# Fewer, wider transfers for stacks, local scores and sums, a planner's clock threshold of 0.5, and new order tables in a four-layer attention kernel

## The chip, the cores and the metric

The kernel runs on one core of one Trainium2 chip. The metric is the device time of one execution in microseconds (us), the median over several runs. All traces are of one profiled execution.

## The reference

Four layers in the order A, B, A, B over x of shape [1, 2048, 512], with 32 heads of 16. Each layer adds the attention of the normalised x to x:

```python
# A: each position sees 8 keys, itself and every second one before it
idx = arange(S)[:, None] - arange(8)[None, :] * 2        # masked where < 0
attn = softmax(where(idx >= 0, q . k[idx] * 16 ** -0.5, -1e9))
oA = (attn . v[idx]) @ wo
# B: each position sees the 256 positions up to itself
p = softmax(where((i - j >= 0) & (i - j < 256), q . k * 16 ** -0.5, -1e9))
oB = (p . v) @ wo
x = x + A(layernorm(x)); x = x + B(layernorm(x))         # twice, same weights
```

Everything is float32.

## The kernel before, in words

The 2048 rows are cut into eight chunks of 256. An A layer and the B layer behind it go through the chunks together, so there are 16 pairs of steps in all, scopes A0, B0 to A15, B15. Matrices are split into a float16 high and a low part, and three products (L1034 to L1036 for transposed results, L1054 to L1057 for others) stand for one float32 product.

In a step of layer A, TensorE makes queries and keys and then local scores for a window of 39 keys per group of 32 rows (L1193). ScalarE copies them out (`keep`, L1202), `shelve` (L1211) writes them to a DRAM copy `sd`, and `band` (L1215) reads the diagonal band back into `l`, from which the softmax of eight weights follows (L1234 to L1251). The weights go through DRAM once more (`ptd`, `ptt`, L1278 and L1285) and meet the values (`vd`, `vs`, L1265 and L1273).

In a step of layer B, queries and keys (s = 0 and s = 1) come out transposed. ScalarE makes the high part `eh` (L1331), VectorE the low part `el` (L1334). Six transfers per operand (`put`, L1344, 128 KB each, z = 0 to 2 by two parities) write them to a DRAM copy `re`, and four `stack` tasks read it into `stk_q` (L1357) or `stk_k` (L1359), with the three parts of a head below each other in 48 rows. Rows 48 to 63 of each half are padding, filled once at the start; two of them in `stk_q` later hold the maxima. The first scores (L1420) run on the stacks. VectorE blanks a triangle (`pick`, L1439) and takes row maxima (L1435), which go through small DRAM tiles `md` (`mput`, L1471, and `mget`, L1477) into the pad rows of `stk_q`. Then the scores are made again with the maxima subtracted (L1571), ScalarE takes the exponentials (L1581, L1593), POOL or VectorE zeroes triangles (L1610, L1604), and the products with the values follow (L1626). At the end of a step the sums are collected from `os` (`gather`, L1700), inverted, sent out (L1710) and read back spread over 16 rows (`spread`, L1715).

What runs when is set by a planner. Every piece of work is a task, `plan.add(engine, us, function, r=reads, w=writes, size=KB, alt=other engine)`. The table `ORDER` holds for each scope and task its place in its engine's queue; a negative place chooses the alternative engine. `Plan.order` (L549) walks the queues with the tasks' assumed times and emits them in the order of their planned starts, so it also decides how the five queues interleave. In it a transfer lands after

```python
dma = max(dma, t.end + 0.9) + t.size / 390.0
landed = dma + 0.9 + SLACK[t.size < 50]
```

and `cool` makes TensorE slower where a stretch of `GRID` = 3.4133 us was filled by less than `LOW`:

```python
h[2] = 1.0 / (1.0 + math.exp((h[0] / GRID - LOW) / EDGE))
```

`RECORDS` corrects the number of profiler records of some tasks; 122 idle tasks of three matmuls (L1763) fill gaps of TensorE. Transfers are issued by SyncE and ScalarE and use eight semaphores in turn, so that a transfer's issue also waits for the transfer eight places before it.

Of the kernel before, what the change touches and what calls it, by code (L numbers as in the profile page):

```python
# [9 lines left out]
F16 = mybir.dt.float16  # L10
# [435 lines left out]
SLOW = 0.25  # L446
LEAVE = {"Q": 0.1, "C": 0.13, "X": 0.18, "V": 0.14, "R": 0.1, "F": 0.095, "": 0.0}
AGAIN = {"PE": 0.0, "DVE": 0.11, "ACT": 0.12, "POOL": 0.055, "SP": 0.0}
GRID, LOW, EDGE = 3.4133, 0.4, 0.03
SLACK = 0.9, 0.45  # L450
SUPPLY = 5.0

# [228 lines left out]
def kernel(  # L681
# [1051 lines left out]
    def zeros(pad):  # L1733
        return pad.t.rearrange("p a b -> p (a b)").bitcast(F16)
# [70 lines left out]
```

## Time and profile before

| | before |
|---|---|
| median of 3 runs | 1408.19 us (1407.26 to 1411.21) |
| profiled execution, own time | 1414.15 us |
| its span | 1412.4 us |
| mean granted TensorE clock | 0.974 |
| busy: PE / PEld / DVE / ACT / POOL | 1308.5 / 841.8 / 852.2 / 825.8 / 405.9 us |
| DMA packets, bytes | 203658, 195.08 MB |

Busy time of an engine counts its instructions but not the issuing of transfers. PE is TensorE's matmuls, PEld its weight loads. The profiled execution took 6 us more than the median of the runs. In the page, a name such as stk_q<-re is a transfer or an operation that writes stk_q from re; SPq and ACTq are the queues of SyncE and ScalarE when they issue transfers.

### The profile page before, as it was taken

The page shows a single profiled execution, that of the slowest core. Times are in us where ns is not written, and L with a number is a line of the kernel's source. Part 1 is how long each engine was busy: PE and PEld are TensorE (multiplying, and loading weights), DVE is VectorE, ACT ScalarE, POOL GpSimd, SP SyncE. Part 2 cuts the span into 40 slices and gives each one's busy share as a digit, 9 for nine tenths or more (in the row PEclk, how much of TensorE's full clock was granted, in tenths as well). Part 3 has the DMA queues.
Part 4 walks back from the last instruction along what each step waited for, and adds up shares of the span by engine and source line. Part 5 has one row for each costly group of instructions (what it writes and reads, how often), then busy time and mean ns, then how long its engine had stood idle before and what let it go on. Part 6 is the DMA issues. An engine that isn't in the chain of part 4 may idle for free.

```text
span 1412.4 us, 62375 instructions
## 1 busy us (share of the span) xinstructions
PE 1308.5 (93%) x27206; PEld 841.8 (60%) x27206; DVE 852.2 (60%) x1932; ACT 825.8 (58%) x1303; POOL 405.9 (29%) x839
## 2 busy tenths in 40 slices
PE   8989999999898999879999898989999898998988
PEld 7766556575475746646566464746656474574645
DVE  5455764755647666374664637566473765748494
ACT  7754657474574746546676373838557364663644
POOL 5260212332221233133223130323242241222232
PEclk9999999999899998999999999999999999999999
DMA  8875544736355373552545546364554636335332
GB/s 261 236 168 162 133 115 135 154 114 171 102 148 134 88 200 92 148 147 86 160 113 152 152 143 158 94 174 125 157 123 134 175 100 155 102 98 147 103 98 67
DMA packets 203658, 195.08 MB, mean 138 GB/s; under 512 B 92892, under 2 KB 147932, under 8 KB 203384
## 3 DMA queue, kind: packets, MB, share of 16 engines
q1 hardware_dynamic: 175096, 170.43, 44.2%
q10 hardware_dynamic: 28288, 20.66, 6.0%
q8 instruction: 213, 3.49, 1.1%
q14 instruction: 61, 0.50, 0.1%
HBM read 94.11 MB, written 79.36 MB: 123 GB/s over the span
## 4 chain that ended last, share of the span: by engine, by line
PE 59%; DMA 11%; DVE 10%; ACT 7%; SPq 4%; issue 4%; POOL 2%; ACTq 1%; DVEq 0%; POOLq 0%
PE banks L1034 7%; PE banks L1626 7%; PE banks L1035 6%; PE banks L1036 6%; PE banks L1056 5%; PE banks L1054 5%; PE banks L1571 4%; PE banks L1057 4%; PE banks L1420 4%; DVE m L1435 3%; PE banks L1193 3%; PE banks L1302 3%; ACT p L1581 2%; DMA stk_q<-re 2%; DVE banks L1439 1%
## 5 line engine op out<-in xcount | busy, mean ns | idle before, releaser
L1435 DVE TENSOR_REDUCE m<-banks 128x2 f32<-128x512 f32 x448 | 302.1, 688 | 8.4
L1581 ACT ACTIVATE p<-banks,sclB 128x896 f32<-128x896 f32 x224 | 221.0, 1007 | 74.3 <-PE banks L1571 51.5
L1439 DVE COPY_PREDICATED banks<-trm,banks 128x128 f32<-128x128 int16 x448 | 124.2, 291 | 120.8 <-PE banks L1420 111.8
L1610 POOL TENSOR_SCALAR_AFFINE_SELECT ps<-ps 64x256 f32<-64x256 f32 x300 | 118.2, 416 | 252.3 <-ACT ps L1593 231.2
L1610 POOL TENSOR_SCALAR_AFFINE_SELECT p<-p 64x256 f32<-64x256 f32 x264 | 103.1, 412 | 214.7 <-ACT p L1581 206.6
L1420 PE MATMUL banks<-stk_k,stk_q 48*64 48x320 f16 (+4 forms) x2560 | 139.5, 274 | 24.5 <-DVE m L1435 7.0
L1571 PE MATMUL banks<-stk_q,stk_k 64*64 64x256 f16 (+3 forms) x3584 | 121.0, 239 | 25.0 <-DMA stk_q<-md 8.4
L1420 PEld LDWEIGHTS <-stk_q 48*64 48x64 f16 x2560 | 65.7, 107 | 107.5 <-issue 94.8
L1571 PEld LDWEIGHTS <-stk_k 64*64 64x64 f16 x3584 | 70.3, 108 | 91.0 <-issue 74.3
L1593 ACT ACTIVATE ps<-banks,sclB 128x768 f32<-128x768 f32 x112 | 100.2, 899 | 40.7 <-PE banks L1571 28.4
L1626 PE MATMUL banks<-p,v 64*32 64x192 f32 (+1 forms) x3584 | 112.6, 355 | 6.1 <-ACT p L1581 1.8
L1202 ACT COPY s<-banks 128x624 f32<-128x624 f32 x64 | 74.7, 1257 | 40.7 <-PE banks L1193 23.1
L1640 DVE TENSOR_TENSOR os<-os,banks 128x256 f32<-128x256 f32 x112 | 45.7, 416 | 83.4 <-ACT os L1643 67.0
L1334 DVE SCALAR_TENSOR_TENSOR el<-banks,eh 128x512 f16<-128x512 f32 x64 | 42.8, 687 | 79.4 <-ACT eh L1331 74.0
L1626 PEld LDWEIGHTS banks<-p,v 64*32 64x32 f32 x3584 | 62.9, 106 | 37.6 <-issue 13.0
L1643 ACT COPY os<-banks 128x256 f32<-128x256 f32 x112 | 40.8, 370 | 70.6 <-PE banks L1626 54.4
L1034 PE MATMUL banks<-xh,wA1h 128*128 128x256 f16 x256 | 72.1, 282 | 4.1 <-ACT v L1369 4.1
L1034 PE MATMUL banks<-xh,wA0h 128*128 128x256 f16 x256 | 71.9, 281 | 0.6 <-ACT v L1369 0.6
L1035 PE MATMUL banks<-xl,wA1h 128*128 128x256 f16 x256 | 71.7, 280 | 0.0
L1036 PE MATMUL banks<-xh,wA1l 128*128 128x256 f16 x256 | 71.5, 279 | 0.0
L1035 PE MATMUL banks<-xl,wA0h 128*128 128x256 f16 x256 | 71.3, 279 | 0.0
L1036 PE MATMUL banks<-xh,wA0l 128*128 128x256 f16 x256 | 71.1, 278 | 0.0
(216 smaller groups left out, 3063.8 us busy)
## 6 DMA issues: line engine op xcount, KB each, us to landing
sd<-s SPq DMA_DIRECT2D x92, 156.0 KB
ptt<-ptd SPq DMA_DIRECT2D x128, 96.0 KB
stk_k<-re SPq DMA_DIRECT2D x128, 96.0 KB
stk_q<-re SPq DMA_DIRECT2D x128, 96.0 KB
vs<-vd SPq DMA_DIRECT2D x64, 156.0 KB
re<-eh SPq DMA_DIRECT2D x75, 128.0 KB
vd<-ve SPq DMA_DIRECT2D x32, 256.0 KB
xm<-y SPq DMA_DIRECT2D x32, 256.0 KB
```

Of the source, the lines that this page charges most:

```text
L1034: nc.tensor.matmul(ps[mp].t[:, i], wh, xh, start=k == 0, stop=False)
L1035: nc.tensor.matmul(ps[mp].t[:, i], wh, xl, start=False, stop=False)
L1036: nc.tensor.matmul(ps[mp].t[:, i], wl, xh, start=False, stop=k == 3)
L1202: nc.scalar.copy(S_.t.rearrange("p k (s r) -> p r s k", r=4)[:, 2 * i : 2 * i + 2], pbs[i].t[:, :, 0 : 8 * WIN].rearrange("p r (s k) -> p ...
L1420: nc.tensor.matmul(o, lhs, k, start=True, stop=True, tile_position=(64 * par, 64 * h))
L1435: nc.vector.tensor_reduce(out=m.t[:, :, u, qb], in_=ps.t[:, :, 0 : 2 * P], op=ALU.max, axis=AX.X)
L1439: nc.vector.copy_predicated(t[:, :, 0:64], trm[:, 0].bitcast(I16).unsqueeze(1).broadcast_to([P, 2, 64]), t[:, :, C : C + 64])
L1571: nc.tensor.matmul(ps.t[64 * h : 64 * h + 64, par, at + x0 : at + x0 + q1 - q0], stk[hf, kt][r, col, k0 : k0 + 64], stk[hf, 0][r, col, q0: ...
L1581: nc.scalar.activation(big.t[:, 2 * i : 2 * i + 2], ps.t[:, :, 0:448], AF.Exp, scale=scl["B", 1])
L1593: nc.scalar.activation(small.t.rearrange("p (i m) x -> p m i x", i=2), ps.t[:, :, 0:384].rearrange("p m (i x) -> p m i x", i=2), AF.Exp, s ...
L1610: E.affine_select(out=v, in_=v, pattern=[[0, 4], [a, 64]], compare_op=op, fill=0.0, base=0, channel_multiplier=-a)
L1626: nc.tensor.matmul(acc.t[32 * mm : 32 * mm + 32, h, q0:q1], vv[r, 17 * (H * blk + hd) : 17 * (H * blk + hd) + 32], x.t[r, mm, x0 : x0 + q1 ...
```

## The change

Four transfers get other shapes, the planner's threshold changes, and all tables of places are new. The counts of transfers fall from 1664 to 1391; TensorE's instructions are the same in kind and number.

```diff
-GRID, LOW, EDGE = 3.4133, 0.4, 0.03
+GRID, LOW, EDGE = 3.4133, 0.5, 0.03
 ...
 ORDER = {
-    "B3": [259, 261, 269, 270, 81, 82, 83, 275, 774, 278, 312, 273, 765, 276, 311, 785, 791, 792, 793, 796, 797, 802,
+    "B3": [257, 259, 266, 267, 80, 81, 82, 272, 774, 278, 316, 270, 764, 273, 313, 790, 792, 793, 799, 800, 801, 802,
 ...
# local scores
-            sd = buf("dram", [4, 32 * (WIN + 1) * H], F32, "sd", f"sd{l}_{c}_{t}")
+            sd = buf("dram", [P, WIN * H], F32, "sd", f"sd{l}_{c}_{t}")
             def shelve(E, S_=S_, sd=sd):
-                for g in range(4):
-                    E.dma_start(sd.t[g, 0 : 32 * WIN * H].rearrange("(q x) -> q x", q=32), S_.t[32 * g : 32 * g + 32].rearrange("p k s -> p (k s)"))
+                E.dma_start(sd.t, S_.t.rearrange("p k s -> p (k s)"))
             def band(E=nc.sync, t=t, sd=sd):
-                E.dma_start(L.t[64 * t : 64 * t + 64].rearrange("p u w s -> p u (w s)"),
-                                  bass.AP(..., ap=[[2 * (WIN + 1) * H, 64], [(WIN + 1) * H, 2], [1, W * H]]))
+                for u in range(2):
+                    E.dma_start(L.t[64 * t : 64 * t + 64, u].rearrange("p w s -> p (w s)"),
+                                  bass.AP(..., ap=[[32 * WIN * H, 4], [2 * (WIN + 1) * H, 16], [1, W * H]]))
-            plan.add("SP", 2.4, shelve, ..., alt=("ACT", 2.4))
-            plan.add("SP", 0.65, band, ...)
+            plan.add("SP", 0.65, shelve, ..., alt=("ACT", 0.65))
+            plan.add("SP", 1.2, band, ...)
# high and low parts of queries and keys
-            re = buf("dram", [4, 16, 3, 2, 2, 2 * C], F16, f"e{s}", f"re{l}_{c}_{s}")
+            n3 = (l // 2 * NCH + c) % 3
+            re, vre, vedge = far_e[s, n3], vfar[s, n3], vpads[s, n3]
                     def put(E, z=z, n=n, par=par, re=re, e=e):
-                        E.dma_start(re.t[:, :, z, par].rearrange("q c u x -> (q c) u x"),
+                        E.dma_start(re[:, par, 16 * z : 16 * z + 16].rearrange("q c (u x) -> q (c u) x", u=2),
                                           e[n].t[:, par].rearrange("p i t -> p (i t)"))
                 def stack(E=nc.sync, j=j, s=s, re=re, hp=hp, t=stk[hf, i]):
-                    src = re.t.rearrange("q c z f u x -> q f (c z) (u x)")
-                    for par in range(2):
-                        x = t[64 * par : 64 * par + 48, 4 * hp : 4 * hp + 4]
-                        ... E.dma_start(x, src[j, par])
+                    x, src = t[:, 4 * hp : 4 * hp + 4], re[j].rearrange("f r x -> (f r) x")
+                    ... E.dma_start(x, src)
-                plan.add("SP", 1.3, stack, r=vre[0] + vre[1], w=[vst[hf, i, hp]], size=225 if s else 192)
+                plan.add("SP", 0.65, stack, r=[*vre[0], *vre[1], vedge], w=[vst[hf, i, hp], *([] if s else [vst[hf, "m", hp]])], size=290 if s else 256)
 ...
+    far_e = {(s, i): far.tile([4, 2, 64, 4 * C], F16, name=f"re{s}_{i}") for s in range(2) for i in range(3)}
# sums
             def gather(E, hf=hf):
-                for m in range(4):
-                    s = 16 * (2 * m + hf)
-                    E.dma_start(rc.t[s : s + 16, 0], s_[32 * m + 16 : 32 * m + 17].rearrange("m (k f) -> m k f", f=64))
+                E.dma_start(rc.t[64 * hf : 64 * hf + 64, 0], s_[16::32].rearrange("m (k f) -> m k f", f=64))
-            plan.add("SP", 2.6, gather, ..., alt=("ACT", 2.7))
+            plan.add("SP", 0.65, gather, ..., alt=("ACT", 0.7))
-        plan.add("SP", 0.4, lambda: nc.sync.dma_start(scr.t.rearrange("m (k f) -> (m k) f", f=64), rc.t[:, 1]), ...)
+        def sums_out(E=nc.sync):
+            for hf in range(2):
+                E.dma_start(scr.t[hf::2].rearrange("m (k f) -> m k f", f=64), rc.t[64 * hf : 64 * hf + 64, 1])
+        plan.add("SP", 0.8, sums_out, ...)
# padding: once into the DRAM copy, not into the stacks
-                        nc.sync.dma_start(stk[hf, i][64 * par + 48 : 64 * par + 64], zeros(pad)[0:16, 0:C]...)
+                nc.sync.dma_start(far_e[k, i][:, :, 48:64].rearrange("q f r x -> r (q f) x"), zeros(pad)...)
```

So the DRAM copy of the parts is no longer a tile of a rotating pool but one of three lasting slots for each operand, with the 16 padding rows in it; a stack is one transfer of 128 rows where it was two of 48. The transfers' destinations change shape: a put's from 64 x 2 x 512 to 4 x 32 x 512. In the changed file, lines from `shelve` on stand one to five lines higher (L1420 becomes L1418, L1471 L1469, L1571 about two higher).

The queue of SyncE around the opening of chunk 3, before. Names end in the tile's number; re_3_1 holds the keys' parts, re_3_0 the queries', sd_4 is the next chunk's local scores:

```order
L1344 DMA re_3_1_5582<-eh_3_1_5543 64x2x512 x3
L1344 DMA re_3_1_5582<-el_3_1_5619 64x2x512
L1211 DMA sd_4_0_5696<-s_4_0_5626 32x1248 x4
L1477 DMA stk_q<-md_2_3_5649 2x1024 x2
L1344 DMA re_3_0_5760<-eh_3_0_5726 64x2x512
L1344 DMA re_3_0_5760<-el_3_0_5741 64x2x512 x2
L1359 DMA stk_k<-re_3_1_5582 48x4x256 x4
L1357 DMA stk_q<-re_3_0_5760 48x1024 x2
```

And now (re_0_175 holds the keys' parts, re_0_172 the queries'):

```order
L1469 DMA md_2_3_5455<-mt_2_3_5444 4x32x32 x2
L1344 DMA re_0_175<-eh_3_1_5446 4x32x512 x2
L1344 DMA re_0_175<-el_3_1_5458 4x32x512
L1357 DMA stk_k<-re_0_175 128x4x256
L1475 DMA stk_q<-md_2_3_5455 2x1024 x2
L1210 DMA sd_4_0_5656<-s_4_0_5571 128x1248
L1344 DMA re_0_172<-eh_3_0_5606 4x32x512 x2
L1344 DMA re_0_172<-el_3_0_5641 4x32x512
L1133 DMA y_1_0_5720<-xm_1_1861 128x512
L1357 DMA stk_k<-re_0_175 128x4x256 x2
L1355 DMA stk_q<-re_0_172 128x1024
```

A stack of keys now stands ahead of the queries' puts, the maxima's transfer moved onto SyncE just ahead of the keys' puts, the local scores are one transfer, and every put has the outermost step 4.

ScalarE at the same place, before:

```order
L1331 ACTIVATE eh_3_1_5543<-banks 128x2x256 x2
L1344 DMA re_3_1_5582<-eh_3_1_5543 64x2x512
L1202 COPY s_4_0_5626<-banks 128x2x8x39
L1344 DMA re_3_1_5582<-el_3_1_5619 64x2x512
L1471 DMA md_2_3_5649<-mt_2_3_5632 4x32x32 x2
L1202 COPY s_4_0_5626<-banks 128x2x8x39
L1643 COPY os_2_1_5701<-banks 128x256
L1331 ACTIVATE eh_3_0_5726<-banks 128x2x256
L1593 ACTIVATE ps_2_4_5739<-banks,sclB_170 128x2x2x192
L1331 ACTIVATE eh_3_0_5726<-banks 128x2x256
L1344 DMA re_3_0_5760<-eh_3_0_5726 64x2x512 x3
```

And now:

```order
L1331 ACTIVATE eh_3_1_5446<-banks 128x2x256 x2
L996 CAST ht_5_0_5493<-xn_5_0_5320 128x512
L1344 DMA re_0_175<-eh_3_1_5446 4x32x512 x2
L1344 DMA re_0_175<-el_3_1_5458 4x32x512
L1591 ACTIVATE ps_2_5_5560<-banks,sclB_170 128x2x2x192
L1202 COPY s_4_0_5571<-banks 128x2x8x39 x2
L1331 ACTIVATE eh_3_0_5606<-banks 128x2x256
L1641 COPY os_2_1_5643<-banks 128x256
L1591 ACTIVATE ps_2_4_5650<-banks,sclB_170 128x2x2x192
L1331 ACTIVATE eh_3_0_5606<-banks 128x2x256
L1344 DMA re_0_172<-eh_3_0_5606 4x32x512 x2
L1344 DMA re_0_172<-el_3_0_5641 4x32x512
```

ScalarE issues three of the keys' six puts where it issued two, and three of the queries' six as before; the maxima's transfer left it, and the local scores are no longer copied between the puts.

More of the change, by code (lines that the diff above doesn't have):

```diff
@@ L41 @@
 ORDER = {
[397 rows of a table removed]
[397 rows of a table added]
 }
-RECORDS = "15:1 40:1 67:1 151:1 275:1 316:-1 317:2 322:1 323:-1 470:1 473:1 492:2 526:2 538:1 550:1 572:1 643:1 675:1 715:1 716:-1 721:-1 722:1 762:1 843:2 892:1 905:1 955:1 986:1 1039:1 1051:1 1190:-1 1191:1 1196:-1 1197:3 1367:1 1473:1 1514:1 1585:1 1665:2 1666:-1 1671:2 1672:-1 1830:1 1911:1 1936:1 1952:2 2140:1 2141:-1 2146:-1 2147:2 2183:1 2187:1 2305:1 2411:2 2423:1 2535:1 2615:-1 2616:1 2621:-1 2622:2 2662:1 2758:1 2780:1 2792:1 2808:1 2833:1 2861:1 2886:1 2939:1 3018:1 3090:2 3091:-1 3096:2 3097:-1 3320:1 3414:1 3426:1 3564:1 3565:-1 3570:2 3571:-1 3729:2 3741:1 3754:1 3782:1 3794:1 3835:1 3847:1 3959:1 4040:-1 4041:2 4046:-1 4047:2 4087:1 4194:1 4204:2 4228:1 4262:1 4296:1 4379:1 4439:3 4440:-1 4445:3 4446:-1 4486:1 4576:1 4604:1 4616:1 4626:1 4657:1 4722:1 4729:1 4775:1 4842:1 4914:1 4915:-1 4920:-1 4921:2 4961:1 5079:1 5091:1 5185:1 5250:1 5337:1 5389:1 5390:-1 5395:2 5396:-1 5436:1 5520:1 5554:1 5619:1 5623:1 5691:1 5713:1 5864:2 5865:-1 5870:2 5871:-1 5907:1 6041:1 6082:1 6147:1 6287:1 6299:1 6339:1 6340:-1 6345:2 6346:-1 6382:1 6516:1 6523:1 6569:1 6579:1 6610:1 6622:1 6635:1 6663:1 6675:1 6754:1 6814:1 6815:-1 6820:-1 6821:2 6861:1 6991:1 7044:1 7150:1 7288:2 7289:-1 7294:2 7295:-1 7453:1 7470:1 7490:1 7518:1 7535:1 7561:1 7583:1 7632:1 7665:1"
@@ new lines @@
+RECORDS = "15:1 40:1 67:1 148:1 235:1 275:1 316:-1 317:2 322:1 323:-1 470:1 482:1 526:1 538:1 675:1 715:1 716:-1 721:1 722:-1 758:1 843:1 892:1 905:1 986:1 1039:1 1051:1 1190:-1 1191:2 1196:2 1197:-1 1355:1 1367:1 1408:1 1420:1 1473:1 1514:1 1526:1 1665:1 1666:-1 1671:-1 1672:3 1708:1 1830:2 1842:1 1858:1 1883:2 1936:1 1989:1 2068:1 2140:-1 2141:2 2146:2 2147:-1 2183:1 2305:1 2317:1 2358:1 2370:1 2411:1 2423:1 2464:1 2543:1 2615:2 2616:-1 2621:-1 2622:3 2758:1 2780:1 2792:1 2814:1 2833:2 2870:1 2898:1 2939:1 3090:2 3091:-1 3096:-1 3097:2 3137:1 3320:1 3361:1 3426:1 3485:1 3564:2 3565:-1 3570:-1 3571:2 3611:1 3741:1 3782:1 3804:1 3900:2 3959:1 4040:2 4041:-1 4046:2 4047:-1 4087:1 4228:1 4296:1 4367:1 4439:2 4440:-1 4445:3 4446:-1 4576:1 4604:1 4616:1 4657:1 4775:1 4854:1 4914:-1 4915:2 4920:2 4921:-1 4961:1 5079:1 5091:1 5185:2 5250:1 5337:1 5389:1 5390:-1 5395:-1 5396:2 5523:1 5554:1 5566:1 5570:1 5619:1 5623:1 5672:1 5713:1 5725:1 5864:1 5865:-1 5870:2 5871:-1 6029:1 6094:1 6147:1 6339:-1 6340:1 6345:-1 6346:2 6382:1 6482:1 6504:1 6516:1 6520:1 6557:1 6591:1 6675:1 6754:1 6773:1 6814:2 6815:-1 6820:2 6821:-1 6857:1 6979:1 6991:1 7138:1 7150:1 7209:1 7288:-1 7289:2 7294:1 7295:-1 7437:1 7453:1 7470:1 7490:1 7518:1 7583:1 7600:1 7632:1 7648:1"
@@ L1205, in layer_a @@
                 plan.add("ACT", 1.15, keep, r=[vpb[i]], w=[vS[i]])
-            sd = buf("dram", [4, 32 * (WIN + 1) * H], F32, "sd", f"sd{l}_{c}_{t}")
+            sd = buf("dram", [P, WIN * H], F32, "sd", f"sd{l}_{c}_{t}")
             vsd = Val(sd)
             def shelve(E, S_=S_, sd=sd):
-                for g in range(4):
-                    E.dma_start(sd.t[g, 0 : 32 * WIN * H].rearrange("(q x) -> q x", q=32), S_.t[32 * g : 32 * g + 32].rearrange("p k s -> p (k s)"))
+                E.dma_start(sd.t, S_.t.rearrange("p k s -> p (k s)"))
             def band(E=nc.sync, t=t, sd=sd):
                 x = sd.t
-                E.dma_start(L.t[64 * t : 64 * t + 64].rearrange("p u w s -> p u (w s)"),
-                                  bass.AP(tensor=x.tensor, offset=x.offset, ap=[[2 * (WIN + 1) * H, 64], [(WIN + 1) * H, 2], [1, W * H]]))
-            plan.add("SP", 2.4, shelve, r=vS, w=[vsd], size=600, alt=("ACT", 2.4))
-            plan.add("SP", 0.65, band, r=[vsd], w=[vL[t]], size=160)
+                for u in range(2):
+                    E.dma_start(L.t[64 * t : 64 * t + 64, u].rearrange("p w s -> p (w s)"),
+                                  bass.AP(tensor=x.tensor, offset=x.offset + u * (WIN + 1) * H, ap=[[32 * WIN * H, 4], [2 * (WIN + 1) * H, 16], [1, W * H]]))
+            plan.add("SP", 0.65, shelve, r=vS, w=[vsd], size=600, alt=("ACT", 0.65))
+            plan.add("SP", 1.2, band, r=[vsd], w=[vL[t]], size=160)
         if c == 0:
@@ L1337, in layer_b @@
                 plan.add("DVE", 0.61, low, r=[vps, ve["h"][mp]], w=[ve["l"][mp]])
-            re = buf("dram", [4, 16, 3, 2, 2, 2 * C], F16, f"e{s}", f"re{l}_{c}_{s}")
-            vre = [[Val(re) for _ in range(3)] for _ in range(2)]
+            n3 = (l // 2 * NCH + c) % 3
+            re, vre, vedge = far_e[s, n3], vfar[s, n3], vpads[s, n3]
             for z, n in enumerate("hhl" if s == 0 else "hlh"):
@@ L1352, in stack @@
                 def stack(E=nc.sync, j=j, s=s, re=re, hp=hp, t=stk[hf, i]):
-                    src = re.t.rearrange("q c z f u x -> q f (c z) (u x)")
-                    for par in range(2):
-                        x = t[64 * par : 64 * par + 48, 4 * hp : 4 * hp + 4]
-                        if s == 0:
-                            E.dma_start(x.rearrange("p a t -> p (a t)"), src[j, par])
-                        else:
-                            E.dma_start(x, src[j, par].rearrange("p (a t) -> p a t", a=4))
-                plan.add("SP", 1.3, stack, r=vre[0] + vre[1], w=[vst[hf, i, hp]], size=225 if s else 192)
+                    x, src = t[:, 4 * hp : 4 * hp + 4], re[j].rearrange("f r x -> (f r) x")
+                    if s == 0:
+                        E.dma_start(x.rearrange("p a t -> p (a t)"), src)
+                    else:
+                        E.dma_start(x, src.rearrange("p (a t) -> p a t", a=4))
+                plan.add("SP", 0.65, stack, r=[*vre[0], *vre[1], vedge], w=[vst[hf, i, hp], *([] if s else [vst[hf, "m", hp]])], size=290 if s else 256)
         for t in range(2):
@@ L1705, in gather_o @@
                     E.dma_start(o.t.rearrange("p g t -> p (g t)")[2 * m + hf :: 8], s_[32 * m : 32 * m + 16])
-            plan.add("SP", 2.6, gather, r=vos[hf], w=[vrc[hf]], size=8, alt=("ACT", 2.7))
+            plan.add("SP", 0.65, gather, r=vos[hf], w=[vrc[hf]], size=8, alt=("ACT", 0.7))
             plan.add("SP", 2.5, gather_o, r=vos[hf], w=[vog[hf]], size=256, alt=("ACT", 2.65))
         plan.add("DVE", 0.47, lambda: nc.vector.reciprocal(rc.t[:, 1], rc.t[:, 0]), r=vrc, w=[vrr])
-        plan.add("SP", 0.4, lambda: nc.sync.dma_start(scr.t.rearrange("m (k f) -> (m k) f", f=64), rc.t[:, 1]), r=[vrr], w=[vscr], size=32)
+        def sums_out(E=nc.sync):
+            for hf in range(2):
+                E.dma_start(scr.t[hf::2].rearrange("m (k f) -> m k f", f=64), rc.t[64 * hf : 64 * hf + 64, 1])
+        plan.add("SP", 0.8, sums_out, r=[vrr], w=[vscr], size=32)
         vbc = Val(os_[1])
@@ L1731 @@
     prep("B")
+    far_e = {(s, i): far.tile([4, 2, 64, 4 * C], F16, name=f"re{s}_{i}") for s in range(2) for i in range(3)}
+    vfar = {k: [[Val() for _ in range(3)] for _ in range(2)] for k in far_e}
+    vpads = {k: Val() for k in far_e}
     def zeros(pad):
-        return pad.t.rearrange("p a b -> p (a b)").bitcast(F16)
+        return pad.t.rearrange("p a b -> p (a b)").bitcast(F16)[0:16, 0 : 4 * C]
     for some in ((0,), (1, 2)):
@@ L1741, in fill, with put @@
             v = zeros(pad)
-            nc.gpsimd.memset(v[0:16, 0:C], 0.0)
+            nc.gpsimd.memset(v, 0.0)
             if some[0]:
-                nc.gpsimd.memset(v[0:2, 0:C], -MC)
+                nc.gpsimd.memset(v[0:2], -MC)
         plan.add("POOL", 0.5, fill, w=[vpad])
-        for hf in range(2):
-            for i in some:
-                def put(hf=hf, i=i, pad=pad):
-                    for par in range(2):
-                        nc.sync.dma_start(stk[hf, i][64 * par + 48 : 64 * par + 64], zeros(pad)[0:16, 0:C].unsqueeze(1).broadcast_to([16, 8, C]))
-                plan.add("SP", 1.3, put, r=[vpad],
-                         w=[vst[hf, i, 0], vst[hf, i, 1], *([] if i else [vst[hf, "m", 0], vst[hf, "m", 1]])], size=64)
+        for i in range(3):
+            def put(i=i, k=min(some[0], 1), pad=pad):
+                nc.sync.dma_start(far_e[k, i][:, :, 48:64].rearrange("q f r x -> r (q f) x"), zeros(pad).unsqueeze(1).broadcast_to([16, 8, 4 * C]))
+            plan.add("SP", 0.65, put, r=[vpad], w=[vpads[min(some[0], 1), i]], size=256)
     plan.begin("W")
```

792 rows, old and new, of the table ORDER are left out of this document.

## The prediction

> **What bounds the kernel now.** I read the page first: busy shares, the slices of the granted clock, the DMA queues and the shares of the chain.
>
> ```profile
> span 1412.4 us, 62375 instructions
> PE 1308.5 (93%) x27206; PEld 841.8 (60%) x27206; DVE 852.2 (60%) x1932; ACT 825.8 (58%) x1303; POOL 405.9 (29%) x839
> ...
> PEclk9999999999899998999999999999999999999999
> ...
> q1 hardware_dynamic: 175096, 170.43, 44.2%
> ...
> PE 59%; DMA 11%; DVE 10%; ACT 7%; SPq 4%; issue 4%; POOL 2%; ACTq 1%; DVEq 0%; POOLq 0%
> ```
>
> TensorE is busy 93% of the span, yet it carries only 59% of the chain. The rest is waits that end just in time: 11% in landing transfers, 5% in SyncE and ScalarE issuing them. So what the change does to TensorE's work matters little (its instructions are the same in kind and number), and what it does to the transfers that TensorE waits for decides. Which these are, the chain by time shows. First the opening of chunk 3, the local scores' copy, a put of the high and low parts, a stack of queries:
>
> ```profile
> 318.05 4.00 DMA sd<-s
> ...
> 323.70 4.11 DMA re<-el
> ...
> 328.28 4.15 DMA stk_q<-re
> ```
>
> Then four openings where a stack of queries runs straight into the first scores (L1420):
>
> ```profile
> 680.05 3.75 DMA stk_q<-re
> 683.81 0.04 issue
> 683.86 0.33 PE banks L1420 x3
> ...
> 842.71 2.53 DMA stk_q<-re
> 845.24 0.04 issue
> 845.28 0.46 PE banks L1420 x7
> ...
> 921.61 5.87 DMA stk_q<-re
> ...
> 1091.16 4.02 DMA stk_q<-re
> 1095.18 0.04 issue
> 1095.22 0.56 PE banks L1420 x3
> ```
>
> The list of waits (waiter, released by: us in total, times, longest) says how often:
>
> ```profile
> PEld L1571 <- DMA stk_q<-md: 11.1, 8, 4.5
> PE banks L1571 <- DMA stk_q<-md: 8.4, 6, 4.2
> PEld L1420 <- DMA stk_q<-re: 6.7, 11, 2.3
> ```
>
> Weight loads of L1420 waited eleven times for a stack, in a kernel of sixteen such openings. So at most five openings have room; given as much room as the longest wait is long (2.3 us), the mean is 5 × 2.3 / 16 = 0.7 us. Put, stack, score is a chain without slack.
>
> **The puts: the same bytes over fewer engines.** The 192 puts (L1344, 128 KB) lose nothing in number, but their destination's outermost step goes from 64 to 4. Whether that matters, a transfer of the kernel before with an outermost 4 tells, md<-mt (L1471, 128 rows of 64 B). Two short stretches, 553.80 to 554.35 us with one md<-mt alone, and 1219.60 to 1222.95 us with os<-scr (128 rows of 4 KB) and one transfer of 128 small rows to the DRAM copy ahead of it:
>
> ```profile
> DMA packets 132, 0.01 MB, mean 15 GB/s; under 512 B 132, under 2 KB 132, under 8 KB 132
> q1 hardware_dynamic: 132, 0.01, 16.2%
> ...
> DMA  1979999898399459939927590000000000003310
> ...
> DMA packets 277, 0.55 MB, mean 164 GB/s; under 512 B 148, under 2 KB 148, under 8 KB 276
> ```
>
> In the first stand 132 packets: 128 rows and four more, the 4-byte notes with which each engine that took part reports. In the second, 148 small ones are 128 rows and 20 notes: sixteen of os<-scr and four of the outermost-4 transfer. So a transfer with four outermost steps runs on four engines, one with 128 on sixteen. The changed puts have four. The Trainium skill, "DMA: Bandwidth & Descriptors", in "Why a DMA increments its semaphore by 16 and not by 1", states this as a rule: the largest number up to 16 that divides the slowest dimension of both sides is the number of engines; the trace agrees (4 and 16 notes). This rule speaks against the change: without it the puts would cost what they did.
>
> What four engines cost: os<-scr gives each of sixteen engines 32 KB, exactly what a put now gives each of four, and its packets fill about 24 of 40 slices of 84 ns, 2.0 us. By the page's q1 row, 170.43 MB in 44.2% of sixteen engines over 1412.4 us is 17.1 KB per us and engine: 1.92 us a put, 0.48 us over sixteen. Each put takes 1.44 us more, and six feed one operand's stacks. The skill's same page, "Bandwidth", has 436 GB/s for sixteen engines; by that a put would take an estimated 1.2 us and the sum below would come out some 20 us lower; no row here shows that rate held.
>
> Puts of one operand leave close together. SyncE's timeline in chunk 3:
>
> ```profile
> 313.11 3.19 SPq L1344 DMA_DIRECT2D re<-eh  x3
> ...
> 322.47 0.53 SPq L1344 DMA_DIRECT2D re<-eh  x1
> 323.11 1.19 SPq L1344 DMA_DIRECT2D re<-el  x2
> 324.40 3.26 SPq L1359 DMA_DIRECT2D stk_k<-re  x4
> 327.87 0.78 SPq L1357 DMA_DIRECT2D stk_q<-re  x2
> ```
>
> Lower bound of the delay: the last two puts queue, 2 × 1.44 = 2.9 us. Upper: all six, 8.6, and 0.3 for the stack's larger bytes (256 KB where two of 96 KB went): 8.9. The last three leave in 1.8 us (322.47 to 324.30); on four engines they need 5.8, so the last lands 5.8 − 1.8 − 0.5 = 3.5 us later than its 0.48 after 324.30, and ScalarE now sends three of the same six beside them. I take 4.5 us. Off this go the room of 0.7 and 0.4 us for a stack that is one issue, not two (0.78 for the pair): 3.4 us × 16 openings = 54. TensorE's stall gives the other engines time that shortens later waits; only part of it, since the chain is 41% their work; I let a third go: **+36** (bounds (2.9 − 1.1) × 16 × 2/3 = 19, and (8.9 − 1.1) × 16 × 2/3 = 83).
>
> **Clock after such stalls.** Two stretches that follow late stacks, of chunks 3 and 10 (columns: stretch, length, busy us of PE, PEld, DVE, ACT, POOL, then granted clock, DMA share, GB/s):
>
> ```profile
> 335.50:338.90 3.40, 3.07 (x17) 1.06 (x17) 1.77 (x4) 1.76 (x2) 1.71 (x5) 0.51 0.50 157
> 929.50:932.90 3.40, 3.40 (x53) 1.48 (x46) 2.86 (x6) 2.43 (x3) 0.82 (x3) 0.50 0.72 213
> ```
>
> A stretch of 3.4 us at half speed loses 1.7 us. Two of sixteen openings have it; with 3 to 5 us more of stall I give half of them one more: 8 × 1.7 = **+14** (0 to 27).
>
> **Transfers behind the puts.** Maxima go out between the puts in nine of sixteen chunks of the changed order, and md<-mt uses the same four engines. L1571 already waits for them (8.4 us in 6 waits). One put's 1.44 in nine chunks is 13; some have room: **+10** (0 to 20). SyncE's queue stands still meanwhile, since stk_q<-md waits there for md.
>
> **Fewer issues.** The issuing engines' rows (shortest, median, longest ns):
>
> ```profile
> L1211 SPq DMA_DIRECT2D sd<-s x92: 302/422/1503, 37.5 to 1272.5; - x92
> L1215 SPq DMA_DIRECT2D l<-sd x32: 536/564/1676, 42.4 to 1280.3; - x32
> L1357 SPq DMA_DIRECT2D stk_q<-re x128: 302/413/1876, 118.5 to 1350.0; - x128
> L1359 SPq DMA_DIRECT2D stk_k<-re x128: 308/436/1938, 114.5 to 1350.9; - x128
> L1700 SPq DMA_DIRECT2D rc<-os x72: 502/589/1667, 190.8 to 1324.0; - x72
> L1710 SPq DMA_DIRECT2D scr<-rc x15: 338/346/1258, 199.2 to 1353.2; - x15
> ```
>
> Where the outer step grows to 128 I take 0.55 us. `shelve`: 32 × (4 × 0.42 − 0.55) = 36 us saved. Stacks: 128 × (0.85 − 0.55) = 38. `gather`: 30 × 3 × 0.59 = 53. `band` adds 32 × 0.56 = 18, `sums_out` 15 × 0.35 = 5. Net 104 us, of 1664 transfers at about 0.5 us, 830: an eighth. The chain holds 5% = 71 us of issuing, an eighth of it: **−9** (0 to −40, if all savings fall on the chain). The local scores' copy in one transfer instead of four lands about 1.1 us sooner (4 × 0.42 − 0.55) where the chain passes it; four or five such places: **−5**. Against that, `band` in two parts, each on four engines (64 KB, 0.96 us where 128 KB took 0.48, and an issue of 0.56 more), lands about 1.0 us later: the term lies between −5 and 0. I take −5, since the chain above passes sd<-s (318.05) and no l<-sd.
>
> **At nothing**: pads written once (12 transfers become 6, at the start beside the weights); the new slots `far_e`, reused only three chunks later. 68 fewer POOL selects and 17 more masks on DVE, both off the chain where they go (POOL 29% busy): ±5. The new order otherwise moves work of the same length: ±15, for TensorE's queue ahead of a chunk's first score got slightly shorter (156 rows where 161 stood in chunk 3), which gives stacks less time, not more.
>
> **Sum.** 36 + 14 + 10 − 9 − 5 = +46 us. The profiled execution took 1414 us: 1460. It stands 6 us above the median of the runs (1408.2), so the prediction is **1454 us**. A change under 0.3% (4 us) can't be told from none.
>
> **Rivals.** *The puts are hidden* (faster): the new order has room for them, the chain no longer passes from stack to score, and only the savings are left: −14, and with the shorter SyncE queue another −8: 1392, or 1386 against the median. It decides if an opening has over 4.5 us between its last put's old landing and its first score. For: the longest stack wait is just 2.3 us, and the issues do fall by a sixth. Against: eleven openings without room, and a put of 2 us that no planner's rate of all engines foresees. Chance 0.17.
>
> *Gain and loss cancel*: the delay at its lower bound (19), no new half-speed stretches, the savings at −14 to −20: 1408 ± 4. Chance 0.07.
>
> *The queue of four engines fills*: six puts of Q stand behind those of K, at the upper bound: 83 + 27 + 20 − 14 = +116: 1530, or 1524. For: SyncE sends K's stacks between, so their packets on the first engines queue too, and each transfer waits for the one eight before it. Against: some 8 us lie between K's and Q's last puts in chunk 3 (316.40 and 324.30). Chance 0.15.
>
> **How the numbers follow.** The forecast has 0.61, and 1415 to 1500 as its own range. The range 1390 to 1525 leaves out about half of the fast rival and half of the full queue, 0.16 together.  Faster by over 0.3%: 0.18; within: 0.05; slower: 0.77.
>
> **What would show it.** Right: puts take four notes each; weight loads of L1418 wait for stk_q<-re in nearly every chunk, 3 us and more; DMA's share of the chain rises above 11%; more stretches at half clock right after; issues of SyncE and ScalarE on the chain below 5%. Wrong: stack waits of L1418 stay near 7 us in total; or the stall is elsewhere, in the maxima or local scores; or the share of TensorE's idle time stays at 7% while the clock rises.

## The result, and the profile after

The changed kernel took 1549.52 us (median of 4 runs, 1548.30 to 1555.36) against 1407.72 us before: 1.102 times as long, 95% interval 1.0974 to 1.1066. Times and ratios here and below leave out runs that took over 1.5% longer than the fastest run of their kernel. The direction, and puts on four engines as the cause, were forecast; the time lies above the range, and above the third rival (1524 us) too. Page of the changed kernel:

```profile
span 1546.6 us, 61983 instructions
PE 1339.3 (87%) x27206; PEld 853.5 (55%) x27206; DVE 865.3 (56%) x1949; ACT 828.4 (54%) x1302; POOL 376.2 (24%) x768
...
PEclk9998899999989989799998999989999999999899
...
q1 hardware_dynamic: 176372, 178.94, 42.5%
...
PE 44%; DMA 29%; DVE 9%; ACT 6%; SPq 4%; issue 4%; POOL 2%; ACTq 1%; DVEq 0%; POOLq 0%
DMA re<-el 12%; PE banks L1624 5%; DMA re<-eh 5%; PE banks L1034 5%; PE banks L1056 4%; PE banks L1035 4%; PE banks L1418 4%; PE banks L1036 4%; PE banks L1054 4%; PE banks L1057 4%; PE banks L1569 3%; PE banks L1302 3%; DMA stk_q<-re 3%; DVE m L1433 3%; DMA l<-sd 2%
```

TensorE's busy time grew by 31 us (1308.5 to 1339.3) for the same instructions, the time in which it was idle by 103 (103.9 to 207.3), so that its share fell from 93% to 87%; the chain's share in transfers rose from 11% to 29%. The puts alone, `re<-el` and `re<-eh`, carry 17%. From the list of waits of the changed kernel:

```profile
DVE el L1334 <- DMA re<-el: 77.0, 8, 11.3
PEld L1418 <- DMA stk_q<-re: 67.8, 14, 8.6
PE banks L1418 <- DMA stk_q<-re: 58.8, 12, 8.4
ACT eh L1331 <- DMA re<-eh: 43.1, 11, 7.8
DVE el L1334 <- DMA re<-eh: 24.6, 3, 9.7
...
PEld L1569 <- DMA stk_q<-md: 6.5, 3, 4.1
```

TensorE waits for stacks in 14 weight loads, up to 8.6 us. Three other rows were not foreseen: ScalarE and VectorE, about to write `eh` and `el`, wait for earlier puts to land, 145 us together (the two wait side by side in part, so the sum is no price). The chain shows why, in the opening of chunk 5 (start, length, what):

```profile
525.10 0.60 ACT eh L1331
...
526.85 6.66 DMA re<-eh
...
534.11 0.60 ACT eh L1331
...
538.67 8.87 DMA re<-el
...
547.56 4.63 DMA stk_q<-re
...
552.23 0.48 PE banks L1418 x4
```

At 525 us the keys' high part is made and its puts leave. The queries' high part goes into the same buffer (the pool `pqk` has two, one taken by the keys' `eh`, one by their `el`). It is made at 534 us, when the keys' four puts of `eh` have landed. Then the queries' six puts queue again, the last for 8.87 us, and only then the stack of queries goes. Here the queue is passed twice in one opening.

The wait for the buffers reaches TensorE too. The projections' results stand in banks, from which `eh` and `el` are made, and matmuls that write into banks now wait for `el`:

```profile
PE banks L1056 <- DVE el L1334: 12.1, 4, 6.0
PE banks L1624 <- DVE el L1334: 6.8, 2, 5.6
...
PE banks L1569 <- DVE el L1334: 5.4, 2, 4.9
PE banks L1402 <- DVE el L1334: 5.2, 1, 5.2
...
PE banks L1034 <- DVE el L1334: 3.3, 1, 3.3
```

These are 33 us in all; the kernel before has no such wait over 0.2 us.

How fast the queue of the puts drains shows in the DMA view of 526.85 to 533.50 us, 40 slices of 0.17 us (busy tenths of sixteen engines, GB/s, packets):

```profile
DMA  1226223122222222322222222222222226899529
GB/s 31 37 25 129 92 86 92 62 62 80 99 99 92 92 92 99 99 86 80 92 92 99 92 99 92 99 92 99 92 99 99 92 92 159 159 273 189 129 99 212
DMA packets 594, 0.68 MB, mean 102 GB/s; under 512 B 16, under 2 KB 575, under 8 KB 593
```

For most of it a flat 2, a quarter of sixteen engines, at 92 to 99 GB/s. Four puts ended in the stretch and left sixteen notes. In the trace's packet records the notes come four at a time, at 528.9, 530.4, 531.6 and 533.0 us. At 95 GB/s a put of 128 KB takes 1.4 us: 23 to 25 GB/s an engine.

The granted clock fell as well:

```profile
core 0: 1546.6 us, clock 0.942
```

Before it was 0.974. The missing shares are 90 and 37 us of a full clock, that is about 180 and 73 us at half speed, in 31 stretches where the kernel before had 14.

### The profile page after: what moved, and what is told of

The parts are those of the page before. It is cut to its first block, busy times and chain, and to the rows that moved or that the text cites. A ratio compares the mean times of both kernels' runs of the same rounds, so it can differ in the third digit from the quotient of the medians.

```text
span 1546.6 us, 61983 instructions
## 1 busy us (share of the span) xinstructions
PE 1339.3 (87%) x27206; PEld 853.5 (55%) x27206; DVE 865.3 (56%) x1949; ACT 828.4 (54%) x1302; POOL 376.2 (24%) x768
## 4 chain that ended last, share of the span: by engine, by line
PE 44%; DMA 29%; DVE 9%; ACT 6%; SPq 4%; issue 4%; POOL 2%; ACTq 1%; DVEq 0%; POOLq 0%
DMA re<-el 12%; PE banks L1624 5%; DMA re<-eh 5%; PE banks L1034 5%; PE banks L1056 4%; PE banks L1035 4%; PE banks L1418 4%; PE banks L1036 4%; PE banks L1054 4%; PE banks L1057 4%; PE banks L1569 3%; PE banks L1302 3%; DMA stk_q<-re 3%; DVE m L1433 3%; DMA l<-sd 2%
## 5 line engine op out<-in xcount | busy, mean ns | idle before, releaser
L1418 PE MATMUL banks<-stk_k,stk_q 48*64 48x320 f16 (+4 forms) x2560 | 139.2, 279 | 80.6 <-DMA stk_q<-re 58.8
L1418 PEld LDWEIGHTS <-stk_q 48*64 48x64 f16 x2560 | 64.9, 109 | 174.4 <-issue 100.0
L1608 POOL TENSOR_SCALAR_AFFINE_SELECT p<-p 64x256 f32<-64x256 f32 x236 | 92.9, 416 | 278.2 <-ACT p L1579 269.2
L1608 POOL TENSOR_SCALAR_AFFINE_SELECT ps<-ps 64x256 f32<-64x256 f32 x260 | 102.2, 415 | 230.9 <-ACT ps L1591 223.1
L1569 PE MATMUL banks<-stk_q,stk_k 64*64 64x256 f16 (+3 forms) x3584 | 122.5, 244 | 25.4 <-ACT os L1641 7.2
L1624 PE MATMUL banks<-p,v 64*32 64x192 f32 (+1 forms) x3584 | 121.2, 370 | 12.8 <-DVE el L1334 6.8
L1334 DVE SCALAR_TENSOR_TENSOR el<-banks,eh 128x512 f16<-128x512 f32 x64 | 42.4, 686 | 160.5 <-DMA re<-el 77.0
L1569 PEld LDWEIGHTS <-stk_k 64*64 64x64 f16 x3584 | 73.7, 110 | 83.2 <-issue 68.4
L1624 PEld LDWEIGHTS banks<-p,v 64*32 64x32 f32 x3584 | 66.5, 109 | 47.4 <-issue 17.7
L1638 DVE TENSOR_TENSOR os<-os,banks 128x256 f32<-128x256 f32 x112 | 45.8, 417 | 70.6 <-ACT os L1641 65.1
L1331 ACT ACTIVATE eh<-banks 128x512 f16<-128x512 f32 x64 | 36.3, 596 | 86.2 <-DMA re<-eh 43.1
L1624 PE MATMUL banks<-ps,v 64*32 64x64 f32 (+1 forms) x3584 | 70.4, 252 | 2.9 <-issue 2.3
```

The source lines that it names most:

```text
L1418: nc.tensor.matmul(o, lhs, k, start=True, stop=True, tile_position=(64 * par, 64 * h))
L1569: nc.tensor.matmul(ps.t[64 * h : 64 * h + 64, par, at + x0 : at + x0 + q1 - q0], stk[hf, kt][r, col, k0 : k0 + 64], stk[hf, 0][r, col, q0: ...
L1608: E.affine_select(out=v, in_=v, pattern=[[0, 4], [a, 64]], compare_op=op, fill=0.0, base=0, channel_multiplier=-a)
L1624: nc.tensor.matmul(acc.t[32 * mm : 32 * mm + 32, h, q0:q1], vv[r, 17 * (H * blk + hd) : 17 * (H * blk + hd) + 32], x.t[r, mm, x0 : x0 + q1 ...
```

## The experiments

Medians, and ratios to the kernel before with their 95% intervals. The kernel before ran beside each group: 1408.42 us beside e1 to e4, 1408.49 beside e5 to e8, 1406.97 beside e9 to e11. The ratios come from the single runs and can differ from those of the medians by 0.3%.

| run | what | us | ratio |
|---|---|---|---|
| e1 | before, puts on four engines | 1544.81 | 1.0998 (1.0935 to 1.1062) |
| e2 | changed, puts on sixteen | 1404.38 | 0.9964 (0.9933 to 0.9995) |
| e3 | as e2, keys' puts on four | 1480.72 | 1.0515 (1.0458 to 1.0572) |
| e4 | as e2, queries' puts on four | 1482.21 | 1.0536 (1.0475 to 1.0598) |
| e5 | before, new sums | 1384.20 | 0.9836 (0.9799 to 0.9874) |
| e6 | before, new local scores | 1390.77 | 0.9869 (0.9820 to 0.9919) |
| e7 | before, single stacks, padding late | 1427.52 | 1.0153 (1.0109 to 1.0198) |
| e8 | before, all transfers, padding late | 1411.33 | 1.0040 (1.0008 to 1.0072) |
| e9 | before, new sums and local scores | 1375.26 | 0.9789 (0.9753 to 0.9825) |
| e10 | as e7, padding early | 1401.01 | 0.9984 (0.9946 to 1.0022) |
| e11 | as e8, padding early | 1386.37 | 0.9861 (0.9824 to 0.9898) |

**e1: the puts' shape alone, in the kernel before.**

```diff
-re = buf("dram", [4, 16, 3, 2, 2, 2 * C], ...)
+re = buf("dram", [4, 2, 3, 16, 2, 2 * C], ...)
-E.dma_start(re.t[:, :, z, par].rearrange("q c u x -> (q c) u x"), ...)
+E.dma_start(re.t[:, par, z].rearrange("q c u x -> q (c u) x"), ...)
-src = re.t.rearrange("q c z f u x -> q f (c z) (u x)")
+src = re.t.rearrange("q f z c u x -> q f (z c) (u x)")
```

> The kernel before with one difference: the DRAM copy of the parts is laid out so that a put's destination has the outermost step 4 (4x32x512) instead of 64; stacks still 2 of 48 rows over sixteen engines, old order, old transfers elsewhere. Theory T (the puts over four engines are nearly the whole loss, the six keys' puts and then the six queries' puts queuing at about 1.4 us each): 1500 to 1570 us, with weight loads of L1420 waiting for stk_q<-re in most openings, and el and eh waiting for re<-eh or re<-el. Rival O (the new order and the other transfers carry most of it, puts about the 46 us of the prediction): 1440 to 1465 us.

It took 1544.81 us, 136 more than the kernel before and nearly as long as the changed kernel. From its waits:

```profile
DVE el L1334 <- DMA re<-el: 37.2, 5, 10.2
ACT eh L1331 <- DMA re<-el: 36.0, 7, 9.1
DVE el L1334 <- DMA re<-eh: 35.0, 4, 11.5
ACT eh L1331 <- DMA re<-eh: 23.8, 5, 5.1
...
PEld L1420 <- DMA stk_q<-re: 18.3, 15, 2.9
```

Data, number of transfers and order are those of before. The packets fall from 203658 to 201354, by 2304: twelve for each of the 192 puts, the notes of the twelve engines that no longer take part. What differs is the outermost step, the place of the rows in the DRAM copy, and the row order inside a stack. Theory T holds in time; but the stack's waits, though in most openings, are short. In the old order most of the loss shows at the buffers (132 us in the four rows above), and some at the maxima: the matmuls of L1571 waited 20.9 us for stk_q<-md, where they had waited 8.4.

**e2: the changed kernel with wide puts.**

```diff
-t = t.rearrange("p a (q u c) -> p u (a q) c", u=2, c=16)            # weight columns of layer B
-h, lo = (x.rearrange("p a (q c u) -> p u (a q) c", u=2, c=16) ...)
+t = t.rearrange("p a (m r c) -> p (a m) r c", m=4, c=16)
+h, lo = (x.rearrange("p a (m c r) -> p (a m) r c", m=4, c=16) ...)
-far.tile([4, 2, 64, 4 * C], F16, ...)
+far.tile([2, 64, 4, 4 * C], F16, ...)
-E.dma_start(re[:, par, 16 * z : 16 * z + 16].rearrange("q c (u x) -> q (c u) x", u=2), ...)
+E.dma_start(re[par, 16 * z : 16 * z + 16].rearrange("c q (u x) -> (c q u) x", u=2), ...)
```

> The changed kernel with one difference: the weight columns of queries and keys stand in another order, so that a put's partitions run over (c q u) and its destination is one block of 128 rows, outermost 128; one transfer of 128 rows per stack as before, same order of all instructions (6 more pad transfers and 24 more short vector operations at the start, an estimated 3 us). Theory T: 1385 to 1415 us. Rival O: 1480 to 1510 us, as only the puts' 46 us go.

1404.38 us: 145 us less than the changed kernel from the puts' shape alone, with the weight columns in the order that it needs. A put's rows lie in one block of the DRAM copy here, in e1 in four and before in 64, so it isn't their lying closer together that made e1 slow. The chain looks as before the change, and the waits for buffers are all but gone:

```profile
PE 61%; DMA 13%; DVE 9%; ACT 7%; issue 4%; SPq 2%; POOL 2%; ACTq 1%; DVEq 0%; POOLq 0%
...
PEld L1418 <- DMA stk_q<-re: 16.8, 11, 4.6
PE banks L1418 <- DMA stk_q<-re: 12.5, 9, 4.1
DVE el L1334 <- DMA re<-el: 4.9, 1, 4.9
ACT eh L1331 <- DMA re<-el: 1.5, 1, 1.5
```

**e3 and e4: one operand's puts narrow.** From e2, the old column order, slot layout and put for s = 1 (e3) or s = 0 (e4) only.

```diff
+narrow = s == 1        # e3: keys; e4: s == 0, queries
-far.tile([2, 64, 4, 4 * C], ...)
+far.tile([4, 2, 64, 4 * C] if narrow else [2, 64, 4, 4 * C], ...)
```

> As the wide variant of the changed kernel, but the keys' puts keep the outermost step 4; the queries' puts are wide. Theory T (the queries' eh and el reuse the two buffers of the keys' eh and el, so the keys' puts hold up the queries' projection results): 50 to 90 us above the wide variant. The prediction's step (only the queries' puts stand in the path, the keys' lie ahead of them): within 10 us of the wide variant.

> As the wide variant of the changed kernel, but the queries' puts keep the outermost step 4; the keys' puts are wide. Theory T: 60 to 100 us above the wide variant, and together with the keys' part about the whole difference of the changed kernel. The prediction's step: nearly the whole difference (120 us or more) comes from these puts alone.

Against e2 the keys cost 76 us and the queries 78, together 154 where both at once cost 145. The prediction's step on the keys is refuted. (In both kernels the lines stand four higher: L1335 is `eh`, L1338 `el`, L1422 the first scores.) From the waits of e3, then of e4:

```profile
DVE el L1338 <- DMA re<-el: 80.8, 9, 11.4
ACT eh L1335 <- DMA re<-eh: 44.5, 10, 8.4
DVE el L1338 <- DMA re<-eh: 24.7, 3, 9.7
...
PEld L1422 <- DMA stk_q<-re: 8.6, 5, 2.5
```

```profile
PEld L1422 <- DMA stk_q<-re: 75.4, 13, 9.9
PE banks L1422 <- DMA stk_q<-re: 70.6, 13, 9.7
```

Narrow keys hold up the buffers, narrow queries the stack. Each alone explains its rows of the changed kernel. TensorE's matmuls waited 35 us for `el` in e3, nearly as in the changed kernel, and hardly at all in e4. That the two buffers are what couples them is read from the waits; a kernel with more buffers wasn't run.

**e5, e6 and e9: sums and local scores alone, and together.** `gather` and `sums_out`, and `shelve` and `band`, are taken into the kernel before as the diff of the change has them.

> The kernel before with the changed gather (one transfer for four) and the sums sent out in two transfers, both with outermost 4; order and all else as before. If the chain's share of issuing falls with the number of issues (48 us less of issuing at one eighth on the chain): 3 to 8 us faster, 1400 to 1405. Rival, hidden: 1406 to 1411. Small transfers on four engines cost little, being 64 rows of 256 B.

> The kernel before with the changed local scores' copy (one transfer of 128 rows for four of 32; the band read in two transfers over four engines). Prediction's step: -5 to 0 us, 1403 to 1408. Rival: the band's 64 KB over four engines land about 1 us later and behind each other, and the softmax of the local layer waits: 3 to 10 us slower.

> The kernel before with the changed sums and the changed local scores' copy together, all else as before. If the two gains (-24 and -13 us at the medians) add up: about 1371 us. If both come out of the same waits: about 1384, no better than the sums alone.

The sums gained 24 us and the local scores 18, more than the 3 to 8 and 0 to 5 expected. Together they gained 32, three quarters of 24 + 18 = 42: the product of the two ratios, 0.971, lies below the interval of e9, so a part came out of the same waits. (The expectation for both went by 13 us for the local scores.) e9 is the fastest kernel here, 1375.26 us. Its clock:

```profile
core 0: 1371.2 us, clock 0.994
```

That is 16 us at half speed where the kernel before had 73. TensorE's same instructions were busy 1286.4 us instead of 1308.5: 22 of the 41 us between the two profiled executions. Where the gather's four issues may have cost time shows in rows of the kernel before on ScalarE, which issued 48 of the 120:

```profile
ACT ht L996 <- DMA rc<-os: 9.8, 1, 9.8
ACT xn L986 <- DMA rc<-os: 8.4, 2, 6.1
ACT mt L1458 <- DMA rc<-os: 7.3, 1, 7.3
ACT ve L1264 <- DMA rc<-os: 6.0, 2, 3.5
ACT ps L1593 <- DMA rc<-os: 5.5, 1, 5.5
ACT v L1369 <- DMA rc<-os: 3.1, 1, 3.1
```

Eight waits of six kinds of ScalarE's operations, 40 us, stood behind those transfers. How much of it reached TensorE isn't shown. In e5 one such row is left:

```profile
ACT v L1369 <- DMA rc<-os: 2.6, 1, 2.6
```

**e7, e8, e10 and e11: single stacks with wide puts, and all transfers, in the old order.**

```diff
 # e7, from the kernel before: put, stack, far_e and weight columns as in e2
 # e10, from e7: padding early
-t.place = min(x.place for x in stacks) - 0.5          # all twelve ahead of the first stack
+t.place = k                                           # places of the old padding tasks: 66, 74, 96, 59, 77, 88
 # e8 and e11: the same two with the new sums and local scores as well
```

> The kernel before with the stacks as one transfer of 128 rows each, the parts' copy in lasting slots and the puts as one block of 128 rows (sixteen engines; weight columns in another order); order, local scores and sums as before. 38 us less of issuing on SyncE, in the path from put to stack: theory 5 to 12 us faster (1396 to 1403). Rival: the larger transfer (256 KB for 192) lands later by what the issue saved: 1406 to 1411.

> The kernel before with all new transfers of the changed kernel, the puts made wide, in the old order with the old threshold. If the new order brings nothing, as the wide variant of the changed kernel: 1400 to 1408. If the new order is what uses the new transfers: 1405 to 1412. If single gains add up: 1388 to 1398.

e7 was slower by 1.5%, outside both expectations, and its trace told that the experiment had a fault of its own: twelve pad transfers ahead of the first stack.

```profile
130.90 13.68 SPq L1755 DMA_DIRECT2D re<-pad  x12
144.68 2.63 SPq L1359 DMA_DIRECT2D stk_k<-re  x2
...
148.63 0.83 SPq L1357 DMA_DIRECT2D stk_q<-re  x2
```

The first stack of queries left at 148.63 us; in the kernel before, the first score was at 121. So e7 and e8 don't answer their question; e10 and e11 write the padding early.

> As the single-stack variant of the kernel before (wide puts in one block, stacks of 128 rows, lasting slots), but with the padding written early: in the first such variant all twelve pad transfers stood ahead of the first stack and the first scores of chunk 0 came 32 us late, while from chunk 1 on it ran 23 us faster. If that reading holds: 1385 to 1395 us. If the stacks themselves cost: 1410 or more.

> All new transfers with wide puts in the old order, padding early. It is the wide variant of the changed kernel with the old order and threshold. If the new order costs time on the chip: 1360 to 1380 us, 25 to 45 us below that variant (1405). If the orders are equal: 1400 to 1408.

e10: single stacks with wide puts bring nothing that can be told (1401.01 us, interval 0.9946 to 1.0022). The reading of e7's later chunks as a 23 us gain did not hold. A reason fits, not tested apart: a stack's issue is saved, but by the semaphore records a stack of 256 KB lands 4.4 us after its issue (median), where one of 96 KB took 2.9 and the second of a pair left 0.4 later. e11: all new transfers in the old order, 1386.37 us, 18 us below e2 by the medians and 15 by the ratios; e2 has the same transfers in the new order. So the order found anew, with its threshold and assumed times, costs 15 to 18 us on the chip.

The change in pieces: new transfers −21 (e11 against before), new order +18 (e2 against e11), puts on four engines +145 (changed kernel against e2). Each piece starts where the one ahead of it ends, so their sum must come out at the whole, +142, and proves nothing. What the pieces rest on is e1: the puts' shape alone costs 136 us in the old order too.

## Why the prediction was wrong

- **Four engines: right.** Sixteen notes for four puts, a flat quarter of the engines, and 2304 packets fewer in e1. The rule of the Trainium skill that was weighed there ("DMA: Bandwidth & Descriptors", "Why a DMA increments its semaphore by 16 and not by 1") agrees with e1 and e2: twelve notes fewer for each put in the one, and the loss gone in the other when the outermost step has 128.
- **The price of a put: too high.** 1.92 us was taken from the mean rate of busy engines; the queue drained a put in 1.4 us, 23 to 25 GB/s an engine. The 436 GB/s for sixteen engines of the Trainium skill ("DMA: Bandwidth & Descriptors", "Bandwidth"), 27 each, is nearer than the row that was used.
- **"Six feed one operand's stacks ... I take 4.5 us": the step that failed.** The delay was counted once for each opening, as if the keys' queue drained beside other work. The queries' `eh` and `el` need the keys' buffers, so the queue is passed twice: 4.8 us a chunk from the keys (76 / 16) and 4.9 from the queries (78 / 16). That the keys' share would be as large stood in no sentence, not even as the upper bound: the kernel before shows two short waits of L1331 for puts (5.1 us for re<-eh, 1.1 for re<-el) and none of L1334. A list of who reuses a transfer's source would have shown it.
- **The 4.5 us itself: near, in part by luck.** By the semaphore records a put landed 2.6 to 2.7 us after its issue before (medians of `eh` and `el`) and 6.5 to 8.2 now, 3.8 to 5.5 later. But with 1.4 us a put, the working for the last three gives 4.2 − 1.8 − 0.5 = 1.9 us instead of 3.5: too dear a put made up for too few puts in the queue.
- **"I let a third go": wrong.** Nothing was absorbed. In e4 the waits of the first scores' matmuls for stacks rose from 12.5 to 70.6 us, by 58 (54 had been worked out before the third went off), and the time by 78.
- **Clock, +14: too small.** TensorE's same instructions were busy 31 us longer than in the kernel before, and 38 longer than in e2 (1301.4 us). The missing clock grew from 32 us in e2 (0.977 of 1405) to 90 (0.942 of 1547), by 57, but not all of it fell on stretches in which TensorE had work.
- **Maxima behind the puts, +10: not seen in the changed order.** L1569's weight loads waited 6.5 us for stk_q<-md and L1509's 6.3, together 12.8, where L1571's had waited 11.1. In the old order (e1) the wait did grow.
- **Fewer issues −9, local scores −5: right in sign, too small.** e9 has −32; all new transfers with wide puts (e11) −21. Pricing them by the chain's 5% of issuing missed the clock, and perhaps what queued behind ScalarE's transfers. In the changed kernel issuing still holds 5% of the chain, where it was to fall below.
- **The new order, 0 ± 15: +15 to +18.** Whether the places or the threshold of 0.5 are the reason stays open; they weren't tried apart.
- **Single stacks, 38 us of issuing: no gain** (e10).

Of the rivals, the full queue came nearest (1524), with its bound of 8.9 us for one operand's six puts; the measured total is 9.1 us a chunk (145 / 16), but it comes from both operands, so the nearness is a coincidence.

## What to carry to other kernels

When a transfer's shape changes, look at the outermost step of both sides before its bytes or its count: here the number of engines followed from it, and 192 transfers with 4 instead of 64 cost 136 to 145 us where the new sums and local scores gained 32. Count the delay of a slower write once for its reader and once for whoever reuses its source buffer; while the transfer is in time, that second wait hardly shows in a list of waits. And try the parts of a bundle alone: two of the four transfers here gained 32 us together, one gained nothing, and one lost 145.

## What the runs showed that was not expected

- Four engines moved 92 to 99 GB/s in 1 KB packets, 23 to 25 GB/s each, about 1.4 times the 17.1 KB per us that an engine moved on average while busy in the kernel before.
- Small savings came with a higher clock: with e9's two edits the granted clock went from 0.974 to 0.994, and the time fell by 32 us where the two terms had been priced at 14.
- The same transfers, with wide puts, ran 15 to 18 us slower in the new order than in the order made for the old ones.
